# Moving the square and the upper-half copy of a weight conversion from ScalarE to GpSimd in a one-core attention and gated-MLP kernel

## The chip, the cores and the metric

The kernel runs on one core of one Trainium2 chip. The metric is the device time of one execution in microseconds (us), taken on the chip: the median of several runs. One further execution is recorded by the hardware profiler, and the profile and the trace come from that one. Engines are named as in the profile: PE (TensorE, the matrix engine, with PEld for its weight loads), DVE (VectorE), ACT (ScalarE), POOL (GpSimd) and SP (SyncE, which here only issues DMAs).

## The reference

Block-causal attention (8 batches, 8 heads, 576 positions, head size 64, blocks of 64) followed by a gated layer with 512 inputs and 1536 hidden columns:

```python
scores = scale * np.matmul(q, k.transpose(0, 1, 3, 2))
scores = np.where(mask, scores, -1000000000.0)      # mask: block_i >= block_j
scores = scores - np.max(scores, axis=-1, keepdims=True)
attn = np.exp(scores)
attn = attn / (np.sum(attn, axis=-1, keepdims=True) + 1e-09)
out = np.matmul(attn, v)
# x: out with heads joined, 4608 tokens x 512
gate = 1.0 / (1.0 + np.exp(-(x @ w_gate)))
val = x @ w_val
return (gate * val @ w_out).astype(np.float32)
```

The inputs of this case reach the core as 64-bit floating-point numbers for the three weight matrices, so the kernel reads each weight as two 32-bit words and makes 32-bit numbers of them itself.

## The kernel before, in words

**Two phases.** The first runs attention over 32 pairs of heads (`attend`, `prep`) and, interleaved on TensorE, the first 512 hidden columns of the gated layer (`mlp1`, four tiles of 128 columns, F1 = 4). The second does the other 1024 hidden columns. The change is in the first.

**One attention pair.** A pair is a list of steps (the tuples FIRST, ALONE, REST and TURN): scores of row block 3 and 2, the tail and the low blocks; for each a maximum on VectorE (line 385, or 425 for the tail) and exponentials on ScalarE (line 388, 427); transposes on TensorE (line 262) and their evictions from PSUM on ScalarE (line 363) or VectorE (line 489); the product with V on TensorE (line 258). The product, the division (line 507) and the split of the result into an upper and a lower part (line 514 on ScalarE, line 519 on GpSimd) of a pair are emitted within the next pair. `prep` makes the queries and keys of the next pair: for the first pairs with transposes on TensorE and evictions on ScalarE (lines 300 and 304), small copies on GpSimd (line 318); for the following ones with transposes on VectorE (line 290), scalings and copies on GpSimd (lines 343, 345, 329, 336).

**The conversion.** The operands of the large products are kept as an upper part of type float32r (`dH`) and the difference to it (`dL`). `convert` makes both from the 64-bit weights, a piece of 128 x 512 numbers at a time: eight pieces for the gate and value weights of the four hidden tiles, four for the output weights. Per piece it issues: the fetch (line 87 or 89, on the DMA queue of SyncE); shift and mask of the high word (line 111, VectorE); the square of the high word read as a float (line 113, ScalarE), which serves as a guard that sets tiny numbers to zero; the sign bits (line 114), the guard itself (line 116), the exponent (line 119) and the weight of the low word (line 120), all on VectorE; their sum (line 121, GpSimd); the rounded copy to the upper part (line 122, ScalarE); the difference as the lower part (line 123, GpSimd).

Buffers: for gate and value pieces the raw words and the intermediate `T_` have two buffers, the square (`cgv[:, 7]`) and the exponent (`cgv[:, 6]`) one each. For output pieces the raw words and the square (`csq`, which shares its two buffers with the tile `ost` of `mlp1`) have two, `T_` one.

**What sets the order.** CONV_PLAN says how many pieces are emitted in which pair: for gate and value two in pair 0 and one in each of pairs 1 to 6, for the output weights one in pairs 5 and 6 and two in pair 7. `mlp1` needs the two pieces of hidden tile f before its matmuls of that tile (line 131), and the four output pieces before those of line 138. The program's scheduler then orders each engine's instructions in its own model of time: of those that are ready it takes the one emitted first. `after` in `convert` ties an instruction behind the last attention instruction of its engine at the time of emission (`behind`, an order without a semaphore): the fetch on SyncE, line 111 on VectorE and line 113 on ScalarE are tied so. Lines 121 to 123 are not. The instructions of each engine stand in its queue in the order that results.

Of the kernel before, what the change touches and what calls it, by code (L numbers as in the profile page):

```python
# [9 lines left out]
F32 = mybir.dt.float32  # L10
F32R = mybir.dt.float32r
U32 = mybir.dt.uint32
AF = mybir.ActivationFunctionType
ALU = mybir.AluOpType
# [28 lines left out]
def attn_glu_kernel(ctx: ExitStack, tc: tile.TileContext, q, k, v, w_gate, w_val, w_out, out):  # L43
    nc = tc.nc
# [25 lines left out]
    def behind(ins, other):  # L70

        tc.add_manual_dep(ins, other.name, mybir.DependencyInfo(mybir.DependencyClass.NoSync,
                                                                mybir.DependencyReason.DATA), reason="order")

    def convert(pieces, tiles, last=None, ahead=False):

        def after(engine, ins):
            if last and engine in last:  # L80
                behind(ins.ins, last[engine])

        def fetch(i):
            src, (raw, *rest) = pieces[i][2], tiles(i)
            chunks = len(src.shape) == 3
            if chunks:
                dma = nc.sync.dma_start(out=raw.rearrange("p (c n) w -> p c (n w)", n=P), in_=src.bitcast(U32))
            else:
                dma = nc.sync.dma_start(out=raw, in_=src.bitcast(U32).rearrange("p (n w) -> p n w", w=2))
            after("SP", dma)  # L90
            return chunks, raw, *rest

        ready = [fetch(0)]
        yield
        if ahead:
            ready.append(fetch(1))
            yield
        for i, (dH, dL, src) in enumerate(pieces):
            chunks, raw, T_, E_, sq = ready.pop(0)
            if not ready and i + 1 < len(pieces):  # L100
                ready.append(fetch(i + 1))

            def like(t):
                return t.rearrange("p (c n) -> p c n", n=P) if chunks else t

            lo, hi = raw[:, :, 0], raw[:, :, 1]
            if E_ is None:
                E_ = hi
            Tf, Ef = T_.bitcast(F32), E_.bitcast(F32)

            after("DVE", nc.vector.tensor_scalar(out=T_, in0=hi, scalar1=3, scalar2=0x3FFFFFF8,
                                                 op0=ALU.logical_shift_left, op1=ALU.bitwise_and))
            after("ACT", nc.scalar.activation(out=sq, in_=hi.bitcast(F32), func=AF.Square))
            nc.vector.scalar_tensor_tensor(out=T_, in0=hi, scalar=0xC0000000, in1=T_,
                                           op0=ALU.bitwise_and, op1=ALU.bitwise_or)
            nc.vector.scalar_tensor_tensor(out=Tf, in0=sq, scalar=TINY_HI * TINY_HI, in1=Tf,
                                           op0=ALU.is_ge, op1=ALU.mult)

            nc.vector.tensor_scalar(out=E_, in0=T_, scalar1=0xFF800000, scalar2=None, op0=ALU.bitwise_and)
            nc.vector.scalar_tensor_tensor(out=Ef, in0=lo, scalar=2.0 ** -52, in1=Ef, op0=ALU.mult, op1=ALU.mult)  # L120
            nc.gpsimd.tensor_add(out=Tf, in0=Tf, in1=Ef)
            nc.scalar.copy(out=dH, in_=like(Tf))
            nc.gpsimd.tensor_sub(out=dL, in0=like(Tf), in1=dH.bitcast(F32))
            yield

# [38 lines left out]
    with ExitStack() as s2:  # L164
# [406 lines left out]
        def conv_out():  # L571
            W_out.append(mp.tile([P, F1, 2, DM], F32R, name="wo"))
            yield from convert([x for f in range(F1) for x in out_w(W_out[0], 0, f, DM)], tiles_o, last)

        conv_gv = convert([x for f in range(F1) for x in gate_val_chunks(wg, wv, f)], tiles_gv, last, ahead=True)
        conv_o = conv_out()
        n_conv = [-1, -1]
# [517 lines left out]
```

## Time and profile before

| | |
|---|---|
| median of 3 runs | 1180.55 us (1180.47 to 1180.87) |
| span of the profiled execution, first to last instruction | 1177.6 us |
| around that span, against the median | 2.95 us |
| DVE, ACT, POOL busy | 776.6, 617.4, 349.6 us |
| squares and copies of `convert` on ACT | 24, from 13.1 to 146.3 us |

Times in the trace count from the span's start. A row of the timeline reads: start, duration, engine, line, operation, output<-input, shape, count, and in brackets the idle time of the engine before it with what ended it. Durations of one engine may overlap a little, since the next instruction starts while the last one drains. A row of stages reads: the stretch, then the busy time of PE, PEld, DVE, ACT and POOL, the granted clock of TensorE (1.00 is full), the share of the DMA engines and GB/s. A row of one line reads: count, shortest/median/longest in ns, first and last start in us, and the shapes.

### The profile page before, as it was taken

Reading aid. Unit: us, or ns where it says so; the run is one execution under the profiler, and the core shown is the slowest. Engines: PE = TensorE matmul, PEld = TensorE weight load, DVE = VectorE, ACT = ScalarE, POOL = GpSimd, SP = SyncE. Lnnn points to the kernel's source line nnn. Section 1 sums busy time; section 2 is a strip of 40 time slices with the busy share of each in tenths; the row PEclk is TensorE's granted clock in tenths of the full one; section 3 lists DMA queues with packets and bytes.
Section 4 is the critical chain, followed back from the end, with each engine's and each line's share of the span. In section 5 each row is a group of like instructions: output and inputs, shape, how many; then the busy total and the mean of one; then the engine's idle time right before and its main releaser. Section 6 shows DMA issues by size and latency. Waiting matters only on the chain.

```text
span 1177.6 us, 19283 instructions
## 1 busy us (share of the span) xinstructions
PE 1153.6 (98%) x6749; PEld 976.3 (83%) x6749; DVE 776.6 (66%) x1405; ACT 617.4 (52%) x1364; POOL 349.6 (30%) x390
## 2 busy tenths in 40 slices
PE   6999999999999999999999999999999999999998
PEld 4555778778777877787889899999999998998997
DVE  5778845454564555457959977867877746746754
ACT  5867766766676676666334443553453422423421
POOL 2345523222331322234002133032033263262330
PEclk8999999999999999999999999999999999999999
DMA  8765434435434443534323236235197455164241
GB/s 198 180 144 115 104 89 100 117 74 127 99 89 112 102 122 71 125 105 134 111 95 126 91 120 223 71 136 202 39 339 276 158 172 179 39 212 132 83 143 54
DMA packets 253361, 153.34 MB, mean 130 GB/s; under 512 B 193232, under 2 KB 215248, under 8 KB 252624
## 3 DMA queue, kind: packets, MB, share of 16 engines
q1 hardware_dynamic: 241600, 132.15, 40.1%
q10 hardware_dynamic: 11280, 18.91, 4.4%
q8 instruction: 53, 0.87, 0.3%
q0 software_dynamic: 384, 1.05, 0.3%
q14 instruction: 44, 0.36, 0.1%
HBM read 104.73 MB, written 47.33 MB: 129 GB/s over the span
## 4 chain that ended last, share of the span: by engine, by line
PE 90%; DVE 5%; ACT 2%; issue 1%; DMA 1%; POOL 0%; SPq 0%; DVEq 0%; ACTq 0%
PE b L875 27%; PE bank L258 14%; PE m L131 14%; PE m L953 11%; PE m L138 7%; PE bank L262 6%; PE b L953 5%; PE bank L131 3%; ACT P L388 1%; PE m L262 1%; PE bank L138 1%; DVE nm L385 1%; DVE XL L765 0%; DMA raw<-in_moe_w_out_dram 0%; DMA rqk<-in_k_dram 0%
## 5 line engine op out<-in xcount | busy, mean ns | idle before, releaser
L875 PE MATMUL b<-XH,w 128*128 128x384 f32 x1344 | 349.2, 335 | 1.2 <-DVE g L921 1.2
L875 PEld LDWEIGHTS b<-XH,w 128*128 128x128 f32 x1344 | 243.9, 188 | 5.2 <-DVE g L921 1.6
L875 PE MATMUL b<-XL,w 128*128 128x384 f32 x672 | 223.5, 335 | 0.0
L388 ACT ACTIVATE P<-bank,nm 128x512 f32<-128x512 f32 (+3 forms) x256 | 132.1, 530 | 68.3 <-DVE nm L385 68.2
L385 DVE TENSOR_REDUCE nm<-bank 128x2 f32<-128x1024 f32 (+3 forms) x128 | 105.4, 823 | 40.7 <-ACT P L388 37.6
L875 PEld LDWEIGHTS b<-XL,w 128*128 128x128 f32 x672 | 126.1, 188 | 1.6
L953 PE MATMUL m<-wo,hH 128*128 128x512 f32 x384 | 125.0, 391 | 0.0
L363 ACT COPY G<-bank 128x768 f32<-128x768 f32 (+3 forms) x140 | 93.2, 694 | 26.2 <-PE bank L262 25.3
L258 PE MATMUL bank<-G,VS 128*64 128x320 f32 (+4 forms) x896 | 93.9, 360 | 0.1
L751 POOL TENSOR_TENSOR XB<-XB 128x384 f32<-128x384 f32 x20 | 20.7, 1037 | 237.9 <-DMA XB<-xT_d 191.6
L138 PE MATMUL m<-wo,hH 128*128 128x512 f32 x256 | 85.4, 398 | 1.4 <-ACT ost L632 1.0
L258 PEld LDWEIGHTS bank<-G,VS 128*64 128x64 f32 x896 | 55.9, 137 | 36.7 <-issue 4.3
L900 ACT ACTIVATE g<-g 128x384 f32<-128x384 f32 x72 | 37.8, 526 | 88.5 <-DVE g L913 48.6
L953 PEld LDWEIGHTS m<-wo,hH 128*128 128x128 f32 x384 | 72.0, 188 | 13.5
L131 PE MATMUL m<-XH,wv 128*128 128x512 f32 x240 | 82.3, 400 | 0.0
L131 PE MATMUL m<-XH,wg 128*128 128x512 f32 x240 | 82.1, 399 | 0.0
L764 ACT CAST XH<-XB 128x1536 fp32r<-128x1536 f32 (+2 forms) x72 | 65.2, 941 | 29.4 <-DVE XB L762 24.1
L765 DVE TENSOR_TENSOR XL<-XB,XH 128x1536 fp32r<-128x1536 f32 (+2 forms) x72 | 75.8, 1084 | 0.0
L262 PEld LDWEIGHTS bank<-ident,P 128*128 128x128 f32 x560 | 65.8, 141 | 11.5 <-ACT P L388 0.8
L953 PE MATMUL m<-wo,hL 128*128 128x512 f32 x192 | 75.2, 392 | 0.0
L262 PE MATMUL bank<-ident,P 128*128 128x128 f32 x560 | 74.8, 273 | 0.1
L409 DVE MEMSET bank<- 64x128 f32 x64 | 10.6, 165 | 88.0 <-PE bank L258 87.3
(183 smaller groups left out, 2339.5 us busy)
## 6 DMA issues: line engine op xcount, KB each, us to landing
xT_d<-xT ACTq DMA_DIRECT2D x32, 288.0 KB
XB<-xT_d SPq DMA_DIRECT2D x16, 576.0 KB
part_d<-ost SPq DMA_DIRECT2D x36, 256.0 KB
VS<-in_v_dram SPq DMA_DIRECT2D x64, 128.0 KB
part_d<-ost ACTq DMA_DIRECT2D x32, 256.0 KB
rqk<-in_k_dram SPq DMA_DIRECT2D x108, 72.0 KB
rqk<-in_q_dram SPq DMA_DIRECT2D x108, 72.0 KB
wgv_d<-st SPq DMA_DIRECT2D x8, 896.0 KB
```

What stands on the lines that cost most here:

```text
L131: mm = nc.tensor.matmul(ps, lhsT=lh, rhs=rh, start=(i == 0), stop=(i == n - 1))
L138: mm = nc.tensor.matmul(ps, lhsT=lh[:, f, t * P:(t + 1) * P], rhs=rh, start=(f == i == 0), stop=(f == F1 - 1 and i == 2))
L258: pe_last[:] = [nc.tensor.matmul(*args, **kw).ins]
L262: pe_last[:] = [nc.tensor.transpose(*args).ins]
L363: mark("ACT", nc.scalar.copy(out=dst, in_=src))
L385: mark("DVE", nc.vector.tensor_reduce(out=nm[:, c0:c0 + 2], in_=ps[:, :, c:c + n], axis=AX.X, op=ALU.max, negate=True))
L388: mark("ACT", nc.scalar.activation(out=Pi[:, h], in_=ps[:, h, c:c + n], func=AF.Exp, bias=nm[:, c0 + h:c0 + h + 1], accum_out=sm[:, 5 * h ...
L764: nc.scalar.copy(out=XO[j][0][:, a:b], in_=x)
L765: sub = nc.vector.tensor_sub(out=XO[j][1][:, a:b], in0=x, in1=XO[j][0][:, a:b].bitcast(F32))
L875: mm = nc.tensor.matmul(ps, lhsT=lh, rhs=rh, start=(first and k == 0), stop=(k == n - 1), skip_group_check=not first)
L900: mark2("ACT", nc.scalar.activation(out=t, in_=c, func=AF.Tanh, scale=0.5))
L953: mm = nc.tensor.matmul(po[t], lhsT=lh[:, f, t * P:(t + 1) * P], rhs=rh, start=(half == 0 and i == 0), stop=(half == 1 and i == 5))
```

## The change

The square of the guard and the copy to the upper part, in all twelve pieces, are issued on GpSimd. The square becomes a product of the high word with itself, and the tie behind the last attention instruction of ScalarE, which the square had, is dropped with nothing in its place. Nothing else is edited; the scheduler orders the program anew.

```diff
             after("DVE", nc.vector.tensor_scalar(out=T_, in0=hi, scalar1=3, scalar2=0x3FFFFFF8,
                                                  op0=ALU.logical_shift_left, op1=ALU.bitwise_and))
-            after("ACT", nc.scalar.activation(out=sq, in_=hi.bitcast(F32), func=AF.Square))
+            nc.gpsimd.tensor_tensor(out=sq, in0=hi.bitcast(F32), in1=hi.bitcast(F32), op=ALU.mult)
             nc.vector.scalar_tensor_tensor(out=T_, in0=hi, scalar=0xC0000000, in1=T_,
                                            op0=ALU.bitwise_and, op1=ALU.bitwise_or)
...
             nc.gpsimd.tensor_add(out=Tf, in0=Tf, in1=Ef)
-            nc.scalar.copy(out=dH, in_=like(Tf))
+            nc.gpsimd.tensor_copy(out=dH, in_=like(Tf))
             nc.gpsimd.tensor_sub(out=dL, in0=like(Tf), in1=dH.bitcast(F32))
```

## The prediction

> **What bounds the kernel now.** I read the page first: the span, the busy shares and the shares of the chain that ended last.
>
> ```profile
> span 1177.6 us, 19283 instructions
> PE 1153.6 (98%) x6749; PEld 976.3 (83%) x6749; DVE 776.6 (66%) x1405; ACT 617.4 (52%) x1364; POOL 349.6 (30%) x390
> PE 90%; DVE 5%; ACT 2%; issue 1%; DMA 1%; POOL 0%; SPq 0%; DVEq 0%; ACTq 0%
> ```
>
> TensorE is busy for 98% of the span and carries 90% of the chain. The three runs have a median of 1180.55 us, so 2.95 us lie around the profiled span of 1177.6; I hold these fixed and sum against the median. What happens beside a busy TensorE costs nothing unless TensorE then waits. The edit touches twelve pieces (eight of the gate and value weights, four of the first output weights), so next I read the stages that hold them.
>
> ```profile
> 40.00:60.00 20.00, 18.23 (x138) 12.12 (x137) 14.37 (x30) 16.70 (x54) 6.77 (x9) 1.00 0.73 170
> 150.00:600.00 450.00, 449.12 (x2936) 356.75 (x2937) 260.40 (x501) 286.47 (x689) 119.44 (x161) 1.00 0.44 109
> ```
>
> After 150 us TensorE is idle for under 1 us in 450. Before it, in attention pairs such as those of 40 to 60 us, TensorE waits 1.8 us in 20, ScalarE is busy for 16.7 and VectorE for 14.4: the pair is a ring of short waits, and a delay of any engine in the ring is a delay of everything behind it. So the edit can act only ahead of 150 us, and what it gains or loses there shifts the rest unchanged.
>
> **The change, part by part. What moves.** The costs, as count: shortest/median/longest ns, from the views of single lines.
>
> ```profile
> L113 ACT ACTIVATE cgv<-cgv x8: 658/672/702, 13.1 to 105.8; 128x512 f32<-128x512 f32 x8
> L122 ACT CAST wg<-cgv x4: 612/618/642, 18.3 to 98.3; 128x512 fp32r<-128x512 f32 x4
> L121 POOL TENSOR_TENSOR cgv<-cgv x8: 1263/1270/1287, 16.4 to 111.2; 128x512 f32<-128x512 f32 x8
> L601 POOL CAST XH<-XH x1: 734/734/734, 553.3 to 553.3; 128x256 fp32r<-128x256 f32 x1
> L336 POOL CAST QBL<-QL x48: 227/234/245, 117.2 to 524.5; 64x64 fp32r<-64x64 f32 x48
> ```
>
> ScalarE loses a square of 0.67 and a copy of 0.62 us per piece: 12 x 1.29 = 15.5 us. GpSimd gains a product of two 128x512 operands, which I price as its sum of that shape, 1.27 us. The copy of 512 elements to fp32r has no row; the nearest casts take 0.234 us for 64 elements and 0.734 for 256, which is 2.6 ns an element, so 0.734 + 256 x 2.6 = 1.40 us. It cannot be below 0.734 and should not pass twice that, 1.47. GpSimd gains 12 x 2.67 = 32 us. The Trainium skill, GPSIMD Engine Reference, section Engine selection, puts one-input operations there at roughly line rate (its section on elementwise cost measures a loop of 512 elements at 0.769 us): by it the copy would be 0.77 us and the last term below +0.1 instead of +0.7 at its worst; the two cast rows speak against it, and the 1.40 stands.
>
> **The queues.** On GpSimd the sum, the copy and the difference of a piece now follow each other with no wait for another engine, 1.27 + 1.40 + 1.28 us in one block. Behind the block stand copies and scalings for the next attention pair, which are wanted some 10 us later. The square had an order constraint on ScalarE; on GpSimd it has none, so it goes as early as its data and its one buffer allow. The data are early, as fetches already are: the two first pieces of the output weights are fetched at 31.48, in the third of 32 pairs.
>
> ```profile
> 31.48 1.07 SPq L89 DMA_DIRECT2D XB<-in_moe_w_out_dram  x2
> ```
>
> The buffer of the squares of gate and value pieces is single, and free when line 116 of the piece before has read it. So I expect the square of piece i+1 on GpSimd right after line 116 of piece i, while VectorE has lines 119 and 120 of piece i still to do. Line 116 itself will not wait: its square is a pair old. No DMA is issued by the moved steps.
>
> **One pair in detail (47 us).** ScalarE, VectorE and GpSimd:
>
> ```profile
> 47.09 0.67 ACT L113 ACTIVATE cgv<-cgv 128x512 f32<-128x512 f32 x1
> 48.12 0.68 ACT L514 CAST XH<-xT 128x576 fp32r<-128x576 f32 x1
> 51.85 0.60 ACT L300 ACTIVATE KQ<-m 128x512 f32<-128x512 f32 x1 [0.85 <-PE m L262]
> 52.34 0.68 ACT L388 ACTIVATE P<-bank,nm 128x512 f32<-128x512 f32 x1
> 48.24 0.69 DVE L116 SCALAR_TENSOR_TENSOR cgv<-cgv 128x512 f32<-128x512 f32 x1
> 49.16 1.41 DVE L119 TENSOR_SCALAR cgv<-cgv 128x512 uint32<-128x512 uint32 x1
> 50.49 1.21 DVE L385 TENSOR_REDUCE nm<-bank 128x2 f32<-128x1024 f32 x1
> 48.88 1.41 POOL L519 TENSOR_TENSOR XL<-xT,XH 128x576 fp32r<-128x576 f32 x1 [6.02 <-ACT XH L514]
> ```
>
> The maximum (line 385) is ready at 51.70, the exponential that needs it starts at 52.34, because line 300 stands before it. ScalarE is late by 0.64 us, and the square's slot (47.09 to 47.66) is 0.57 of that. Taken out, the exponential starts at 51.77: -0.57 us. The other side is line 119: it takes 0.42 us undisturbed and 1.41 here, because the GpSimd subtraction of line 519 runs from 48.88. VectorE and GpSimd do not overlap in these instructions; about 1 us is the price of one GpSimd instruction meeting one of VectorE's. The Trainium skill, SBUF — State Buffer, section Who interferes with whom, says why: a VectorE instruction with two SBUF inputs, or in a two-port mode, and a GpSimd instruction lock each other out for the whole instruction. The trace agrees (+0.99 us), and this is the rule that speaks against the change.
>
> Now line 519 waits only for line 514, which comes 0.57 earlier, so it starts at 48.3, level with line 116 at 48.24. If line 116 is first, the square falls mainly under the maximum, which reads PSUM and was not stretched (1.21): the pair gains 0.57. If line 519 is first, line 116 waits until some 49.6 and ends at 50.3; then the square starts at once, line 119 follows 0.23 us later (49.16 less the end of line 116, 48.93) and waits about 1 us; the maximum ends near 52.9 and the exponential is 0.6 later than now. This pair: -0.57 or +0.6, taken as 0.
>
> The pairs before and after it:
>
> ```profile
> 35.42 0.69 DVE L116 SCALAR_TENSOR_TENSOR cgv<-cgv 128x512 f32<-128x512 f32 x1
> 37.59 1.21 DVE L385 TENSOR_REDUCE nm<-bank 128x2 f32<-128x1024 f32 x1
> 39.28 0.68 ACT L388 ACTIVATE P<-bank,nm 128x512 f32<-128x512 f32 x1
> 35.82 1.56 POOL L519 TENSOR_TENSOR XL<-xT,XH 128x576 fp32r<-128x576 f32 x1 [6.20 <-ACT XH L514]
> 61.13 0.69 DVE L116 SCALAR_TENSOR_TENSOR cgv<-cgv 128x512 f32<-128x512 f32 x1
> 64.60 0.69 ACT L388 ACTIVATE P<-bank,nm 128x512 f32<-128x512 f32 x1 [1.54 <-DVE nm L385]
> 61.53 1.55 POOL L519 TENSOR_TENSOR XL<-xT,XH 128x576 fp32r<-128x576 f32 x1 [5.60 <-ACT XH L514]
> ```
>
> At 35 us line 519 moves from 35.82 to 35.25, ahead of line 116 at 35.42: the second order. ScalarE's slack was 39.28 - 38.80 = 0.48, so the net is between -0.2 (no square behind) and +0.65; taken +0.6. At 61 us line 519 moves to 60.96, again ahead of 61.13. ScalarE waits 1.54 us for VectorE there, so nothing is gained: +0.2 to +1.0, taken +0.9. The three pairs together: +1.5.
>
> **The start.** The square of the first piece and the one at 19.57:
>
> ```profile
> 13.12 0.70 ACT L113 ACTIVATE cgv<-cgv 128x512 f32<-128x512 f32 x1
> 13.86 0.69 DVE L116 SCALAR_TENSOR_TENSOR cgv<-cgv 128x512 f32<-128x512 f32 x1 [1.68 <-ACT cgv L113]
> 19.57 0.66 ACT L113 ACTIVATE cgv<-cgv 128x512 f32<-128x512 f32 x1
> 20.65 1.11 PE L262 MATMUL m<-ident,rqk 128*128 128x128 f32 x4 [3.00 <-ACT G L363]
> 19.50:20.00 0.50, 0.00 (x0) 0.00 (x0) 0.50 (x1) 0.50 (x3) 0.50 (x1) 0.50 0.83 185
> 29.50:30.00 0.50, 0.50 (x5) 0.40 (x6) 0.00 (x0) 0.34 (x2) 0.13 (x1) 0.96 0.61 171
> ```
>
> VectorE waits 1.68 us for the first square; without that, lines 116, 425, 119 and 120 come earlier and the second softmax block with them: 0.57 us for the slot of the square, some 0.6 for VectorE's wait. The second square's slot, up to 0.55, lies right ahead of the eviction for which TensorE waits 3.00 us. TensorE would resume some 1.7 us earlier, near 18.9. But the granted clock fell to half near 19.3 and came back near 29.5; if it comes back when it did, 1.7 us of work that ran at full clock now runs at half, which gives back a third to a half. Bounds -1.8 and -0.6; taken -1.2.
>
> **Later pairs.**
>
> ```profile
> 78.27 1.23 DVE L385 TENSOR_REDUCE nm<-bank 128x2 f32<-128x1024 f32 x1
> 79.43 0.62 ACT L122 CAST wv<-cgv 128x512 fp32r<-128x512 f32 x1 [1.73 <-POOL cgv L121]
> 79.97 0.68 ACT L388 ACTIVATE P<-bank,nm 128x512 f32<-128x512 f32 x1
> 96.99 0.69 ACT L388 ACTIVATE P<-bank,nm 128x512 f32<-128x512 f32 x1 [2.60 <-DVE nm L385]
> 112.52 0.62 ACT L122 CAST wv<-cgv 128x512 fp32r<-128x512 f32 x1 [0.94 <-POOL cgv L121]
> 114.58 1.21 PE L258 MATMUL bank<-KQ,QB 128*128 128x288 f32 x4 [1.36 <-issue]
> ```
>
> At 79.43 the copy, late for want of GpSimd's sum, holds the exponential until 79.97, though the maximum was ready at 79.50: -0.45 without it, +0.75 for the square meeting line 119: +0.3. At 112.52 the same (-0.45), and there is no next square; TensorE's 1.36 us wait at 114.58 follows from that exponential. At 96.99 ScalarE waits 2.60 us for VectorE, so only the collision counts, 0 to +0.9, taken +0.5. Together +0.35.
>
> **The last output piece.**
>
> ```profile
> 145.00 1.30 POOL L121 TENSOR_TENSOR XB<-XB 128x512 f32<-128x512 f32 x1 [0.63 <-DVE XB L120]
> 147.01 0.50 PE L138 MATMUL m<-wo,hH 128*128 128x512 f32 x1 [0.25 <-ACT wo L122]
> ```
>
> TensorE waits 0.25 us at 147.01 for ScalarE's copy of the last piece, right behind the sum of 145.00 to 146.31. On GpSimd the copy ends at 147.7 instead of 146.96: +0.7, or 0 where the pieces ahead finish earlier because their copies no longer wait in ScalarE's queue; taken +0.4.
>
> **Sum:** -1.2 + 1.5 + 0.35 + 0.4 = +1.05, that is 1180.55 + 1.05 = 1181.6 us. The bounds of the terms (start -1.8 to -0.6, the three pairs -0.57 to +2.25, later -0.9 to +0.75, last 0 to +0.7) rarely meet at one end. What a measurement of this kernel can tell from no change is 0.2%, 2.4 us. So the forecast is: no change that can be told, 1179.5 to 1183.5.
>
> **Rivals.** *The squares miss VectorE (faster).* If they are queued where VectorE reads PSUM (before the pair's line 111, or under the maximum), the pairs give -0.2, -0.57 and +0.2, the later ones -0.9, and with the start and the last piece the sum is -2.3: 1178.3. For it: GpSimd is idle in most of a pair. Against it: the buffer comes free just at line 116. Chance 0.22.
>
> *The clock holds (faster).* The half clock covered 19.3 to 29.5, behind a wait of 3.00 us. With that wait nearer 2.2 us, or with the recovery one step earlier, TensorE does some 5 of those 10 us of work in half the time: another -2.5, so 1179.1. Against it: TensorE is then still idle for over 2 us at that place. Chance 0.13.
>
> *GpSimd is backed up when VectorE converts (slower).* The place is lines 114 to 120 in the five pairs from 34 to 97 us: with a second GpSimd instruction waiting behind line 519 each time, be it a square of this kind of weights or one of the output weights, VectorE is locked out twice per piece. The price, on top of the forecast: the pairs at 47 and 90 us at their worse ends (+0.6 and +0.4), and one more meeting in each of the five, 0.9 less the 0.23 of other work between two such lines, 5 x 0.67 = 3.35; in all +4.35, 1185.9. It decides as soon as GpSimd's queue holds two ready instructions when line 114 begins. Chance 0.15.
>
> *The relief never reaches the path.* ScalarE's freed 15.5 us all fall where it waits for maxima anyway, and the collisions fall beside TensorE's work: 1180.5. Chance 0.05.
>
> **How the numbers follow.** The forecast keeps 0.45. Faster by over 2.4 us takes half of the first rival (0.11), somewhat under half of the second (0.06) and 0.05 of the forecast: 0.22. Slower takes most of the third (0.13) and three tenths of the forecast (0.14): 0.27. The rest, 0.51, is no change. Range: 1177.6, where both faster rivals partly hold, to 1186.0, which is the slower one.
>
> **What would show it.** Right: on GpSimd a product of 1.27 us directly after line 116 of the piece before, a copy near 1.4; more of lines 116, 119 and 120 stretched past 1.3 us than now; the exponentials of the pairs at 47 and 79 us no longer behind lines 300 and 122; TensorE back before 19.5 us. Wrong: the products far from line 116, a copy near 0.8, no new stretched lines, a half clock that is gone or short, or a changed order of the attention work, which the program's scheduler makes anew and which I cannot see from here.

## The result and the profile after

| kernel | median of its runs | runs |
|---|---|---|
| before | 1180.51 us (1177.65 to 1180.87) | 4 |
| after | 1186.76 us (1185.66 to 1187.78) | 4 |

The changed kernel takes 1.006 of the time of the one before (95% interval 1.0045 to 1.0074): it is slower by 0.6%, 6.25 us, and lies 0.8 us above the predicted range. The profiled execution took 1185.66 us, 1.76 us of it outside the span. Other executions on record have about as much outside theirs, so of the 2.95 us that were set beside the span before, some 1.2 us is an estimate of how far that profiled execution lay below its median. The two profiles differ by 6.3 us, as the medians do.

First the page of the changed kernel (span and busy shares).

```profile
span 1183.9 us, 19282 instructions
PE 1155.7 (98%) x6749; PEld 977.8 (83%) x6749; DVE 778.3 (66%) x1405; ACT 605.1 (51%) x1340; POOL 369.8 (31%) x414
```

Then its views of line 113 and line 122 (count, shortest/median/longest ns, first and last start).

```profile
L113 POOL TENSOR_TENSOR cgv<-cgv x8: 1041/1068/1433, 7.8 to 93.6; 128x512 f32<-128x512 f32 x8
...
L122 POOL CAST wg<-cgv x4: 610/611/611, 13.1 to 97.8; 128x512 fp32r<-128x512 f32 x4
```

The moved work is cheaper on GpSimd than I had priced it: 0.61 us a copy and 1.04 to 1.07 us a square. GpSimd is busy for 20.2 us more (369.8 less 349.6), not for 32. The kernel is slower all the same, so the price of the work is not what decides.

Where the time went is seen in the table of stages, which gives per stretch the busy time of PE, PEld, DVE, ACT and POOL and then the granted clock. Before:

```profile
0.00:40.00 40.00, 29.19 (x155) 17.95 (x155) 23.56 (x48) 25.19 (x70) 10.49 (x24) 0.87 0.83 198
40.00:100.00 60.00, 54.99 (x356) 35.58 (x356) 47.31 (x91) 43.93 (x123) 25.15 (x26) 1.00 0.63 143
100.00:135.00 35.00, 33.20 (x224) 23.00 (x224) 26.86 (x52) 28.14 (x75) 18.19 (x19) 1.00 0.48 111
135.00:160.00 25.00, 23.60 (x162) 17.84 (x159) 17.86 (x32) 16.73 (x39) 12.70 (x16) 1.00 0.46 110
```

The same stretches after:

```profile
0.00:40.00 40.00, 29.52 (x165) 18.11 (x166) 24.26 (x51) 24.15 (x72) 17.04 (x31) 0.96 0.82 199
40.00:100.00 60.00, 52.22 (x344) 33.67 (x342) 47.69 (x87) 37.02 (x104) 34.19 (x35) 1.00 0.61 141
100.00:135.00 35.00, 34.26 (x222) 24.24 (x222) 24.78 (x47) 24.76 (x67) 20.75 (x24) 0.96 0.49 113
135.00:160.00 25.00, 20.90 (x127) 14.88 (x124) 19.97 (x36) 13.39 (x33) 14.24 (x18) 0.86 0.38 84
```

TensorE loses a stretch's length less its busy time (it idles), and its busy time times what the clock lacks of 1.00 (it works at half speed for part of it). From 0 to 40 us that is 10.81 + 29.19 x 0.13 = 14.6 us before and 11.7 after: a gain of 2.9, mainly in the clock. From 40 to 100 us it is 5.0 and 7.8, a loss of 2.8; from 100 to 135, 1.8 and 2.1; from 135 to 160, 1.4 and 4.10 + 20.90 x 0.14 = 7.0, a loss of 5.6. The four make +5.8 of the 6.1 us by which all later pairs are shifted. So there are three things to explain: a gain at the start, a loss of some 3 us in the pairs with gate and value pieces, and a loss of over 5 us in one place around 145 us.

For all kernels I use one ruler: the start of the product with V (line 258, `bank<-G,VS`) in each pair, less its start in the kernel before. In the pairs that stand at 133.7 and 152.2 us in the kernel before, the rows of the changed kernel are these.

```profile
134.59 2.93 PE L258 MATMUL bank<-G,VS 128*64 128x320 f32 x28
158.33 1.03 PE L258 MATMUL bank<-G,VS 128*64 128x320 f32 x6
```

That is +0.9 at the first and +6.1 at the second, and from there on the shift hardly changes in any kernel (by 0.3 us at most up to the end, in e11 by 0.9). Each row of the table is one execution, the profiled one, and the level at the start is not the edit's alone: e12 has the order of the kernel before on TensorE, VectorE, ScalarE and GpSimd up to 107 us and stands at +1.2 there all the same, and e2 and e10, with the same order up to 112 us, stand at +1.2 and -1.6 at 30 us. So it is the steps along a row that are read, more than its levels. In e11 the product at 134 us runs in two parts, at 130.43 and 135.74; the table has the first.

| us later than before, in the pair at | 30 | 43 | 56 | 70 | 86 | 103 | 119 | 134 | 152 | end |
|---|---|---|---|---|---|---|---|---|---|---|
| after | -1.8 | -2.0 | -0.7 | +0.1 | -0.3 | +2.2 | +1.5 | +0.9 | +6.1 | +6.3 |
| e1, squares alone | -0.3 | +0.8 | +1.2 | +3.6 | +4.3 | +5.2 | +6.0 | +6.0 | +6.8 | +7.0 |
| e2, copies alone | +1.2 | +1.2 | +1.2 | +1.0 | +0.7 | +0.7 | +0.3 | +0.8 | +5.9 | +6.0 |
| e3, after + tied squares | -1.7 | -1.5 | -1.1 | -1.1 | -1.5 | -1.5 | -2.4 | -2.4 | +1.7 | +1.8 |
| e4, tie in output pieces only | -0.3 | +0.2 | +0.6 | +2.7 | +3.1 | +5.6 | +4.8 | +4.7 | +8.8 | +9.1 |
| e5, e3 with output copies on ScalarE | -2.6 | -2.8 | -2.1 | -2.2 | -2.6 | -2.6 | -3.5 | -2.3 | -0.7 | -0.6 |
| e6, e3 with two T_ | -2.2 | -2.2 | -1.1 | -1.1 | -1.5 | -1.5 | -1.7 | -2.2 | +0.5 | +0.7 |
| e7, gate and value pieces only | -2.6 | -1.5 | -1.1 | +1.2 | +1.5 | +3.9 | +3.2 | +3.5 | +3.4 | +3.4 |
| e8, output pieces only | +0.3 | +1.0 | +0.5 | +0.5 | +0.5 | +0.5 | +1.0 | +0.6 | +4.6 | +4.7 |
| e9, e3 in gate and value pieces only | -0.3 | -0.3 | +0.1 | +0.1 | -0.3 | -0.3 | -1.2 | -0.9 | -0.9 | -0.8 |
| e10, e2 with an added order | -1.6 | -0.5 | -0.5 | -0.7 | -1.0 | -1.0 | -1.5 | +1.3 | +0.7 | +0.9 |
| e11, e3 with an added order | -2.6 | -2.3 | +1.0 | +1.0 | +0.6 | +0.6 | -0.3 | -3.2 | +1.8 | +2.7 |
| e12, before with two T_ | +1.2 | +1.2 | +1.2 | +1.2 | +1.2 | +1.2 | +2.6 | +6.5 | +5.1 | +5.4 |

The step from 134 to 152 us is the clearest in it: every kernel with the output pieces' copies on GpSimd and no order added loses 2.7 to 5.2 us there (after, e2, e3, e4, e6, e8); those with only their squares on GpSimd lose 0.8 and 1.6 (e1, e5); those that leave the output pieces as they were lose nothing (e7, e9).

### The profile page after: what moved, and what is told of

Read it like the earlier page. It is cut to its first block, busy times and chain, and to the rows that moved or that the text cites. A ratio compares the mean times of both kernels' runs of the same rounds, so it can differ in the third digit from the quotient of the medians.

```text
span 1183.9 us, 19282 instructions
## 1 busy us (share of the span) xinstructions
PE 1155.7 (98%) x6749; PEld 977.8 (83%) x6749; DVE 778.3 (66%) x1405; ACT 605.1 (51%) x1340; POOL 369.8 (31%) x414
## 3 DMA queue, kind: packets, MB, share of 16 engines
q0 software_dynamic: 384, 1.05, 0.3%
## 4 chain that ended last, share of the span: by engine, by line
PE 91%; DVE 3%; DMA 2%; issue 1%; ACT 1%; SPq 1%; POOL 0%; DVEq 0%; ACTq 0%; POOLq 0%
PE b L875 29%; PE m L131 14%; PE bank L258 14%; PE m L953 11%; PE m L138 7%; PE bank L262 6%; PE b L953 5%; PE bank L131 3%; PE bank L138 1%; ACT P L388 1%; DVE nm L385 1%; SPq L228 0%; PE m L262 0%; DMA XB<-in_moe_w_out_dram 0%; DMA r_d<-rT 0%
## 5 line engine op out<-in xcount | busy, mean ns | idle before, releaser
L329 POOL TENSOR_SCALAR KQ<-KQ 128x128 f32<-128x128 f32 x24 | 13.3, 556 | 177.6 <-DVE KQ L290 177.6
```

## The experiments

Medians are compared with runs of the kernel before on the same chip. The theories at first: by the *queue theory* (from e5 on, the *order theory*) the loss comes from where the moved instructions stand in GpSimd's queue: squares right behind line 116, and the difference of an output piece too far back. By the *load theory* it comes from the time that they take on GpSimd, wherever they stand. By the *ScalarE theory* it is ScalarE's new order.

| | median us | before us | ratio (95%) |
|---|---|---|---|
| e1 | 1185.01 | 1179.55 | 1.0049 (1.0037 to 1.0062) |
| e2 | 1183.45 | 1179.55 | 1.0033 (1.0021 to 1.0046) |
| e3 | 1182.25 | 1179.55 | 1.0021 (1.0013 to 1.003) |
| e4 | 1186.71 | 1179.55 | 1.006 (1.0046 to 1.0074) |
| e5 | 1180.17 | 1179.17 | 1.001 (1.0001 to 1.0018) |
| e6 | 1180.41 | 1179.17 | 1.0013 (1.0004 to 1.0021) |
| e7 | 1181.98 | 1179.17 | 1.0026 (1.0015 to 1.0038) |
| e8 | 1183.56 | 1179.17 | 1.0034 (1.0022 to 1.0046) |
| e9 | 1178.19 | 1179.68 | 0.9986 (0.9978 to 0.9995) |
| e10 | 1180.88 | 1179.68 | 1.0011 (1.0002 to 1.0019) |
| e11 | 1181.34 | 1179.68 | 1.0012 (1.0003 to 1.0021) |
| e12 | 1184.74 | 1179.68 | 1.0037 (1.0024 to 1.0051) |

**e1 and e2: each half alone.** e1 keeps the copy on ScalarE, e2 the square (with its tie):

```diff
e1:
-            nc.gpsimd.tensor_copy(out=dH, in_=like(Tf))
+            nc.scalar.copy(out=dH, in_=like(Tf))
e2:
-            nc.gpsimd.tensor_tensor(out=sq, in0=hi.bitcast(F32), in1=hi.bitcast(F32), op=ALU.mult)
+            after("ACT", nc.scalar.activation(out=sq, in_=hi.bitcast(F32), func=AF.Square))
```

> Only the square on GpSimd, the copy on ScalarE. Queue theory (the loss comes from the place of the square in GpSimd's queue: ahead of line 123 while its own words are still on the way, and beside line 119): nearly the whole loss, 1184.5 to 1187. Load theory (the loss grows with GpSimd's added busy time, 12.5 us from squares and 7.3 us from copies): about two thirds, 1183.5 to 1185. ScalarE theory (the relief was worth something and the copy lost it): under 1182.

> Only the copy on GpSimd, the square on ScalarE with its tie. Queue theory: no loss, 1179.5 to 1181.5, since the copy stands between the sum and the difference and holds nobody up. Load theory: a third of the loss, 1182 to 1183.

Measured: 5.5 and 3.9 us more than before. Both halves cost by themselves, and at different places: e1 loses its 6 us step by step up to 134 us, e2 its 5 us in the one step after it. The queue theory, which had put all of the loss on the squares, missed e2: there is a second cause. The load theory, with 1185 and 1183 as its upper ends, was nearer to both. The ScalarE theory falls with e1.

**e3 and e4: the square's place.** The square is ordered behind the difference (line 123) of the piece before, in all pieces or in the output pieces alone. Nothing is taken off GpSimd.

```diff
-            nc.gpsimd.tensor_tensor(out=sq, in0=hi.bitcast(F32), in1=hi.bitcast(F32), op=ALU.mult)
+            square = nc.gpsimd.tensor_tensor(out=sq, in0=hi.bitcast(F32), in1=hi.bitcast(F32), op=ALU.mult)
...
+            if i: behind(square.ins, lower.ins)
...
-            nc.gpsimd.tensor_sub(out=dL, in0=like(Tf), in1=dH.bitcast(F32))
+            lower = nc.gpsimd.tensor_sub(out=dL, in0=like(Tf), in1=dH.bitcast(F32))
e4:
+            if i and not chunks: behind(square.ins, lower.ins)
```

> The changed kernel with each square tied on GpSimd's queue behind line 123 of the piece before. Queue theory: the squares meet neither line 119 nor a difference that waits, so the loss goes: 1179.5 to 1181.5. Load theory: same GpSimd work, 1185.5 to 1187.5.

> The same tie for the four pieces of the output weights alone. Queue theory: the lag that arises behind 124 us (from +1.7 to +6.1) goes, the one before it stays: 1181.5 to 1183.5. Load theory: 1185.5 to 1187.5.

e3 is 2.7 us above the kernel before and not 6.25; at 134 us it is even 2.4 us ahead. e4 is as slow as the changed kernel, where the load theory had it and the queue theory had not; the place of the output pieces' squares is not what their loss comes from. What e3 saves and e4 does not belongs to the place of the gate and value squares. How, is seen in the timeline of one pair. After, VectorE from line 111 to the maximum (line 385), with GpSimd:

```profile
45.88 0.42 DVE L111 TENSOR_SCALAR cgv<-cgv 128x512 uint32<-128x512 uint32 x1
...
47.12 1.72 DVE L116 SCALAR_TENSOR_TENSOR cgv<-cgv 128x512 f32<-128x512 f32 x1
49.07 1.18 DVE L119 TENSOR_SCALAR cgv<-cgv 128x512 uint32<-128x512 uint32 x1
50.16 1.21 DVE L385 TENSOR_REDUCE nm<-bank 128x2 f32<-128x1024 f32 x1
...
46.75 1.54 POOL L519 TENSOR_TENSOR XL<-xT,XH 128x576 fp32r<-128x576 f32 x1 [2.07 <-ACT XH L514]
48.92 1.04 POOL L113 TENSOR_TENSOR cgv<-cgv 128x512 f32<-128x512 f32 x1 [0.63 <-DVE cgv L116]
```

The same pair in e9 (below), where gate and value squares are tied as in e3:

```profile
46.89 0.42 DVE L111 TENSOR_SCALAR cgv<-cgv 128x512 uint32<-128x512 uint32 x1
...
48.14 1.70 DVE L116 SCALAR_TENSOR_TENSOR cgv<-cgv 128x512 f32<-128x512 f32 x1
50.07 0.40 DVE L119 TENSOR_SCALAR cgv<-cgv 128x512 uint32<-128x512 uint32 x1
50.40 1.19 DVE L385 TENSOR_REDUCE nm<-bank 128x2 f32<-128x1024 f32 x1
```

Line 116 is held up by line 519 in both. Line 119 is held up only where the square stands right behind line 116: 1.18 us against 0.40. From line 111 to the maximum it takes 4.28 us against 3.51, 0.77 more for this one meeting. In a later pair the meeting has a consequence of its own. After:

```profile
94.04 1.26 DVE L119 TENSOR_SCALAR cgv<-cgv 128x512 uint32<-128x512 uint32 x1
...
93.60 1.42 POOL L113 TENSOR_TENSOR cgv<-cgv 128x512 f32<-128x512 f32 x1 [1.32 <-DVE cgv L116]
...
99.12 1.90 PE L258 MATMUL bank<-KQ,QB 128*128 128x288 f32 x4 [1.94 <-ACT P L388]
```

TensorE in e9, and then the stage from 100 to 105 us after the change:

```profile
98.21 1.21 PE L258 MATMUL bank<-KQ,QB 128*128 128x288 f32 x4 [1.10 <-POOL wg L122]
```

```profile
100.00:105.00 5.00, 5.00 (x24) 3.56 (x24) 2.88 (x6) 3.49 (x8) 3.58 (x4) 0.71 0.80 136
```

TensorE waits 1.94 us where it waits 1.10 in e9, and then has a mean clock of 0.71 from 100 to 105 us: that is 5.00 x 0.29 = 1.45 us more, an estimate from this row. The 0.84 of the wait and the 1.45 are nearly all of the ruler's step of +2.5 from 86 to 103 us; e9 has no step there.

**e7 and e8: the two kinds of pieces.** The whole change, untied, in the gate and value pieces alone (e7) or in the output pieces alone (e8); the other kind has lines 113 and 122 as before.

```diff
e7 (e8 with "not chunks"):
+            nc.gpsimd.tensor_tensor(out=sq, in0=hi.bitcast(F32), in1=hi.bitcast(F32), op=ALU.mult) if chunks else after("ACT", nc.scalar.activation(out=sq, in_=hi.bitcast(F32), func=AF.Square))
...
+            (nc.gpsimd.tensor_copy if chunks else nc.scalar.copy)(out=dH, in_=like(Tf))
```

> The change in the eight gate and value pieces alone (untied squares, copies on GpSimd); the four output pieces as before. Order theory: the two losses are apart. What the gate and value pieces cost is there by 134 us (the changed kernel was +0.9 us at that point), and no jump follows: 0 to 2 us more than the kernel before. Load theory: eight of twelve pieces bring two thirds of the loss of 6.3 us: 4.2 us more.

> The change in the four output pieces alone; the gate and value pieces as before. Order theory: the jump between 134 and 152 us is whole: 4 to 6 us more than the kernel before (nothing gained at the start either). Load theory: four of twelve pieces bring one third of the loss of 6.3 us: 2.1 us more.

Measured: 2.8 and 4.4 us more. The four output pieces cost more than the eight others, against the load theory, and they do so in the one step after 134 us. e7 came out 0.8 us above what the order theory allowed; its eight executions lie between 1179.75 us, at a mean granted clock of 1.000, and 1184.98, at 0.994, so that whether a half-clock stretch follows differs here from one execution to the next.

**What happens at 145 us.** After the change, GpSimd, VectorE, ScalarE and TensorE around the third and fourth output pieces:

```profile
140.78 0.61 POOL L122 CAST wo<-XB 128x512 fp32r<-128x512 f32 x1
142.26 0.53 POOL L336 CAST QBH<-QH 64x64 fp32r<-64x64 f32 x2 [0.36 <-ACT QH L328]
142.88 1.68 POOL L123 TENSOR_TENSOR wo<-XB,wo 128x512 fp32r<-128x512 f32 x1
...
144.59 0.43 DVE L111 TENSOR_SCALAR XB<-XB 128x512 uint32<-128x512 uint32 x1 [1.18 <-POOL wo L123]
145.78 1.79 DVE L116 SCALAR_TENSOR_TENSOR XB<-csq,XB 128x512 f32<-128x512 f32 x1
147.67 1.32 DVE L119 TENSOR_SCALAR XB<-XB 128x512 uint32<-128x512 uint32 x1
148.91 1.21 DVE L385 TENSOR_REDUCE nm<-bank 128x2 f32<-128x1024 f32 x1
...
151.74 0.61 PE L258 MATMUL bank<-KH,QBH 128*128 128x288 f32 x1 [3.38 <-ACT P L388]
```

And before:

```profile
135.98 1.28 POOL L123 TENSOR_TENSOR wo<-XB,wo 128x512 fp32r<-128x512 f32 x1 [1.28 <-ACT wo L122]
137.58 0.54 POOL L329 TENSOR_SCALAR KQ<-KQ 128x128 f32<-128x128 f32 x1 [0.32 <-DVE KQ L290]
...
137.34 0.38 DVE L111 TENSOR_SCALAR XB<-XB 128x512 uint32<-128x512 uint32 x1
145.14 1.22 DVE L385 TENSOR_REDUCE nm<-bank 128x2 f32<-128x1024 f32 x1
```

Before, the difference of the third piece stood ahead of lines 329 and 336 of the next pair; after, it stands among them, between the two copies of line 336. It frees the only `T_` of the output pieces.

That is not the whole delay. The sum of the third piece starts at 139.40 us after and at 133.41 before, so most of the delay is there already, and part of it comes from the second piece's difference. After:

```profile
133.40 1.04 POOL L113 TENSOR_TENSOR csq<-XB 128x512 f32<-128x512 f32 x1 [2.98 <-DMA XB<-in_moe_w_out_dram]
134.40 1.27 POOL L123 TENSOR_TENSOR wo<-XB,wo 128x512 fp32r<-128x512 f32 x1
...
135.71 0.43 DVE L111 TENSOR_SCALAR XB<-XB 128x512 uint32<-128x512 uint32 x1 [1.98 <-POOL wo L123]
```

Before:

```profile
127.54 1.30 POOL L123 TENSOR_TENSOR wo<-XB,wo 128x512 fp32r<-128x512 f32 x1
...
128.88 0.43 DVE L111 TENSOR_SCALAR XB<-XB 128x512 uint32<-128x512 uint32 x1 [0.47 <-POOL wo L123]
```

The fourth piece's untied square stands ahead of the second piece's difference and waits 2.98 us for its fetch; the difference waits behind it, and line 111 of the third piece waits for the difference. That square alone does not decide either. In e3 the tie puts each square behind a difference; by the ruler e3 is 2.4 us ahead at 134 us, but its third sum starts at 133.42 us, no earlier than before the change, and its third difference, among the same lines, at 137.37 instead of 135.98. In e2, with its squares on ScalarE, lines 116 to 120 of the third piece stand behind a maximum for which VectorE waits 3.61 us, and follow from 135.70 us on. What these kernels share is that the differences of the output pieces come later, and with them the piece behind; the place among lines 329 and 336 is the last part of it.

So, after the change, line 111 of the fourth piece starts at 144.59 and not at 137.34, four of that piece's five VectorE lines stand in one block right ahead of the next maximum, two of them stretched by GpSimd, and the maximum is at 148.91 instead of 145.14. TensorE waits 3.38 us for the exponential behind it, and is then at a clock of 0.86 on the mean of 135 to 160 us.

**e5, e6 and e10: three ways to mend it.** e5 is e3 with the output pieces' copies on ScalarE; e6 is e3 with two buffers for their `T_`; e10 is e2 with nothing but an order: line 329 behind the last difference, up to that of the third output piece (`lowers` lists the differences as they are emitted).

```diff
e5:
+            (nc.gpsimd.tensor_copy if chunks else nc.scalar.copy)(out=dH, in_=like(Tf))
e6:
-            return (co[0][:, j:j + 1024].rearrange("p (n w) -> p n w", w=2), co[1][:, :512], None,
+            return (co[0][:, j:j + 1024].rearrange("p (n w) -> p n w", w=2), co[1][:, 512 * (i % 2):512 * (i % 2) + 512], None,
e10:
-                nc.gpsimd.tensor_scalar_mul(KQ[:, 1, :P], KQ[:, 1, :P], scale)
+                behind(nc.gpsimd.tensor_scalar_mul(KQ[:, 1, :P], KQ[:, 1, :P], scale).ins, lowers[min(len(lowers), 11) - 1])
```

> e3 with one edit: the copies of the four output pieces are back on ScalarE; the copies of gate and value and all squares stay on GpSimd, the squares tied as in e3. Order theory: the loss between 134 and 152 us comes from the place of the third output piece's difference (line 123), which with the copy on GpSimd stands behind the next pair's lines 329 and 336; with the copy on ScalarE it stands ahead of them again, so the jump of +4 us goes and the lead of 2.4 us that e3 has at 134 us lasts to the end: 2.4 us less than the kernel before (1.0 to 3.0 less), a ratio of 0.998. Load theory: the loss is the time that the copies and products take on GpSimd and in which VectorE is locked out; of that 0.61 x 4 us goes back to ScalarE, so the time stays within 1 us of e3: 1.5 to 2.7 us more than before.

> e3 with one edit: the output pieces get two buffers for the intermediate T_, so line 111 of the fourth piece does not wait for the difference of the third. The orders on TensorE and SyncE are those of e3, on GpSimd nearly (line 123 of the third piece still behind lines 329 and 336); only VectorE's changes. Order theory by way of the buffer: lines 111 and 114 of the fourth piece run early, the maximum ahead of which they stood starts 1.5 to 3.5 us earlier, and the time is 1 to 2.5 us less than before. If the rest of the block (lines 116, 119, 120 and the two lockouts) is enough to delay the maximum, half of it stays: about the kernel before. TensorE theory: the loss is in the new order of lines 138 and 262 on TensorE, which stays: e3's time, 2.7 us more than before. Load theory: the same as e3.

> e2 (copies alone on GpSimd) with one added order: line 329 of a pair stands on GpSimd behind the last difference (line 123) emitted, up to that of the third output piece. Nothing is taken off GpSimd. The scheduler then puts line 111 of the third output piece under the maxima again, as before the change. Order theory: the jump of 5 us between 134 and 152 us goes: 0 to 1.5 us more than the kernel before. Load theory: the copies take as long as in e2, so e2's 3.9 us more stay.

Measured: +1.0, +1.2 and +1.2 us. e10 speaks most plainly against the load theory: the copies take as long on GpSimd as in e2, and 2.7 of e2's 3.9 us are gone by an order alone (which makes the scheduler change the order on the other engines too). In e2:

```profile
140.17 0.53 POOL L329 TENSOR_SCALAR KQ<-KQ 128x128 f32<-128x128 f32 x1
142.14 1.29 POOL L123 TENSOR_TENSOR wo<-XB,wo 128x512 fp32r<-128x512 f32 x1
```

In e10:

```profile
135.28 1.29 POOL L123 TENSOR_TENSOR wo<-XB,wo 128x512 fp32r<-128x512 f32 x1
136.70 1.06 POOL L329 TENSOR_SCALAR KQ<-KQ 128x128 f32<-128x128 f32 x1
```

The step from 134 to 152 us, +5.0 in e2, is -0.6 in e10. But e10 has a new loss one pair earlier, +2.8 from 119 to 134 us, where the added order brings TensorE to a wait that e2 hasn't:

```profile
128.17 0.37 PE L258 MATMUL bank<-KH,QBH 128*128 128x288 f32 x1 [1.95 <-ACT P L388]
```

The granted clock is 0.66 from 130 to 135 us behind it. From 119 to 152 us e10 so loses 2.2 us and e2 5.6; the rest of their distance in the table was there at 30 us, while their orders were still the same.

The order theory's sizes were too good, though. It had expected e5 at 2.4 us less than before. In e5 the difference is back ahead of line 329, but a square still stands between the two, and line 111 of the fourth piece meets it:

```profile
135.73 1.05 POOL L113 TENSOR_TENSOR csq<-XB 128x512 f32<-128x512 f32 x1
...
135.85 1.21 DVE L111 TENSOR_SCALAR XB<-XB 128x512 uint32<-128x512 uint32 x1
```

1.21 us instead of 0.38. And the profiled execution of e5, 0.6 us ahead of the kernel before, was the fastest of its eleven. In e6, 2.7 of e3's 4.0 us between 134 and 152 us remain. The second buffer lets line 111 of the fourth piece run at 131.71, but e6 also keeps the tie, so the fourth piece's square stands behind the third piece's difference, and line 116 waits for the square:

```profile
141.66 0.69 DVE L116 SCALAR_TENSOR_TENSOR XB<-csq,XB 128x512 f32<-128x512 f32 x1 [1.90 <-POOL csq L113]
```

So e6 takes one of two ways away by which the difference holds up the fourth piece, and does not tell what the wait for `T_` is worth alone. TensorE's order in e6 is that of e3 throughout, so the 1.3 us less between 134 and 152 us are not a matter of that.

**e9, e11 and e12: the change without its losses, and a control.** e9 has the change with tied squares in the gate and value pieces, and the output pieces as before. e11 is e3 with the order of e10: all 24 instructions on GpSimd, and both losses meant to go. e12 is the kernel before with the two buffers of e6.

> The change with tied squares in the eight gate and value pieces alone; the four output pieces as in the kernel before. In e5 the fourth output piece's square still stood on GpSimd at 135.73 us and line 111 met it (1.21 us instead of 0.38), which is 0.8 of the 1.5 us that ScalarE was ahead there. Order theory: with that square on ScalarE nothing is lost between 134 and 152 us, and the lead of 1.5 to 2.4 us stays: 1.5 us less than the kernel before (0.7 to 2.4 less). Load theory: 16 of the 24 moved instructions still load GpSimd; not below the kernel before, 0.5 to 2 us more.

> e3 (the whole change, squares tied behind the difference of the piece before) with the added order of e10: all 24 instructions stay on GpSimd. Order theory: both losses go and the gain of the start stays: 0 to 2.4 us less than the kernel before. Load theory: e3's 2.7 us more stay.

> A control for e6: the kernel before with two buffers for T_ of the output pieces. In its trace line 111 of the fourth piece waits for nothing (137.34 us), so by the order theory the second buffer brings nothing here: within 1 us of the kernel before. If it is 1.5 us less, the gain of e6 over e3 is the buffer's own and says nothing of the change.

e9 gave what was expected: 1.5 us less than the kernel before (interval 0.6 to 2.6 us), so it beats both kernels; at 134 us it is 0.9 ahead in its profile and stays so. It also makes the cleanest pair of all: e7 and e9 have the same order on TensorE, VectorE and ScalarE from the first instruction to the last, and differ on GpSimd alone, in where the gate and value squares stand. That place is worth 2.8 + 1.5 = 4.3 us. e11 is 1.7 us slower than before, not faster. In its profiled execution it is 2.3 us ahead at 43 us and 1.0 behind at 56, with a mean clock of 0.94 between 40 and 100 us; why that stretch of half clock comes is open. It meets the wait that e10 has, too:

```profile
129.35 0.37 PE L258 MATMUL bank<-KH,QBH 128*128 128x288 f32 x1 [1.95 <-ACT P L388]
```

From 145 to 160 us TensorE idles 1.5 us in e11 and 1.4 before, both at full clock, so the loss at 145 us is gone there; the added order has put another in its place.

e12 missed most, and says most. It adds no work anywhere and takes a possible wait away, and is 5.1 us slower. With a second `T_` the fourth piece's lines run at once behind the third's:

```profile
129.21 1.27 DVE L111 TENSOR_SCALAR XB<-XB 128x512 uint32<-128x512 uint32 x1
...
132.29 1.59 DVE L116 SCALAR_TENSOR_TENSOR XB<-csq,XB 128x512 f32<-128x512 f32 x1
...
135.23 1.21 DVE L385 TENSOR_REDUCE nm<-bank 128x2 f32<-128x1024 f32 x1
```

Four of the piece's lines (111, 114, 116 and 119, with 1.27, 1.67, 1.59 and 1.33 us) are stretched by GpSimd's work and stand ahead of a maximum, which in the kernel before starts at 127.00 us. It is the loss of 145 us again, one pair earlier and with nothing moved to GpSimd; another 1.4 us of step comes from 103 to 119 us. By these timelines, what costs is a piece's block of VectorE lines between GpSimd's instructions and ahead of a maximum, whichever edit brings it there; no run moves that block alone. It also follows that e6 can't be read as "the buffer alone" for a second reason: the buffer changes the order by itself.

## Why the prediction was wrong

The sum was +1.05 us, the result +6.25. Step by step:

- *What bounds the kernel, and where the edit can act*: right. From 160 to 1170 us TensorE is busy for 1008.67 us after and 1008.77 before, and the shift no longer changes.
- *What moves*: the copy was mis-sized, 0.61 us where I took 1.40 and called 0.734 the lowest possible. The casts that I scaled have 64 and 256 elements, and the one of 512 is shorter than that of 256. The one row of 256 (0.734, at 553.29 us) ran beside VectorE's line 754, which ended at 553.78, so it may hold a meeting like those priced in the same prediction; no run shows that cast undisturbed. The rule of the Trainium skill (GPSIMD Engine Reference, section Engine selection: one-input operations at roughly line rate), which I had turned down for those rows, was on the right side. (With the 0.77 us that the prediction set beside it, its last term would have been +0.12, not "below +0.1".) The square was 1.04 and not 1.27. Both errors made the change look dearer than it was, and it was slower nevertheless.
- *The queues*: the squares' place was right in three of the eight gate and value pieces, directly behind line 116, 0.08 us after its end in the pair at 47 us. "As early as its data allow" had a price that was not foreseen: six of the twelve squares stand at the head of GpSimd's queue before their words are there, with waits of up to 7.84 us (at 36.29 us). e4, which ties the output squares, is no faster, so this does not decide. **The step that failed** is the other sentence, that the sum, the copy and the difference follow each other in one block with no wait, and that behind it stand copies "which are wanted some 10 us later". I had asked who waits behind the block, and not what comes in between. With the copy on GpSimd the scheduler puts lines 329 and 336 between the third output piece's copy and its difference, and a square that waits for its fetch between the second's; and the difference is what line 111 of the next output piece waits for. In place of a block with no wait, the runs show +4.0 to +5.2 us between 134 and 152 us where the copies of the output pieces are on GpSimd (e8, e3, e4, e2 and after). Before the change that wait did not show: the difference ended at 137.26 us and line 111 began at 137.34.
- *The last output piece*: taken +0.4 with bounds of 0 and +0.7, for TensorE's wait for the last copy at 147.01 us. Measured: +5.2 (after), +5.1 (e2), +4.0 (e8). The term had the right place and the wrong waiter: it was the maximum ahead of that copy that came late, by 3.8 us, and the half clock behind it cost about as much as TensorE's added waiting (2.9 and 2.7 us in the stage from 135 to 160).
- *The pairs at 35, 47 and 61 us*: taken +1.5 together. The ruler goes from -1.8 at 30 us to +0.1 at 70 us, +1.9. The mechanism, the double meeting that was described, is there at 47 and 61 us; that the sum is near is in part luck, since the pairs came out at -0.2, +1.3 and +0.8 where +0.6, 0 and +0.9 were taken. One more meeting was priced at 0.67 us in the third rival and is worth 0.77 in the pair at 47 us.
- *Later pairs*: taken +0.35, measured -0.4, +2.5 and -0.8 in the pairs at 79, 97 and 112 us (the ruler's steps from 70 to 119 us), +1.4 together. The meeting at 97 us was foreseen (0 to +0.9); the half clock behind it was not.
- *The start*: taken -1.2 within -1.8 and -0.6, measured -1.8 in the one profile. The eight profiles with the gate and value squares and copies on GpSimd lie between -2.6 and -0.3 at 30 us, the three with both on ScalarE (before, e8, e12) between 0 and +1.2, so the gain is shown, but its size only roughly. The assumption that the clock would come back when it did, near 29.5 us, was wrong, as the stage after the change shows:

```profile
25.00:30.00 5.00, 4.76 (x33) 3.34 (x35) 2.77 (x6) 4.16 (x14) 2.99 (x5) 1.00 0.55 169
```

  The rival in which the clock holds was half right, and its gain was lost again by 103 us.

Of the rivals, that GpSimd is backed up when VectorE converts (1185.9 us) came nearest in size. Its place, 34 to 97 us, bore +4.0 by 103 us in the ruler (from -1.8 to +2.2), near its 4.35, though a good part by the half clock; but the start's gain had paid for some of that, and the loss that decides, the step after 134 us, has another cause. Its number was near by chance.

The first theory of the runs fell too: it held the squares for the whole cause. What is shown now: the place of the untied gate and value squares (e7 against e9, whose orders differ in nothing else) and the late difference of the output pieces (e2, e3, e8, e10) are two separate causes, and the sixteen gate and value instructions save some 1.5 us net on GpSimd if both are avoided (e9). What stays open: what is left of e5, 1.0 us above the kernel before, of which the meeting at 135.85 us is a part; of e10 and e11, 1.2 and 1.7 us above, the wait of 1.95 us that the added order brings is a part. How the second cause divides between the wait for `T_`, the lockouts of VectorE and the half clock is not shown run by run.

## What to carry to other kernels

When work is moved to another engine, follow the last instruction of the moved chain in the new queue, see what can get in between it and its forerunner, and ask which buffer it frees and who waits for that buffer; what the instruction costs is the smaller question. In a kernel whose order a scheduler makes, an edit is a new order: here a second buffer alone cost 5 us. If a moved instruction is wanted in a certain place, tie it there: with the gate and value squares untied the edit cost some 3 us (e7), and with them behind the difference the same work saved 1.5 us (e9).

## What the runs showed of the hardware

A rounding copy of 128x512 to fp32r took 0.61 us on GpSimd, less than one of 128x256 in the kernel before (0.734, beside a VectorE instruction), and about as long as on ScalarE (0.618). The product of a tile with itself took 1.04 us, the sum of two tiles of that shape 1.27.

The length of TensorE's wait alone did not tell whether the clock falls. Behind 1.94 us (after, at 99.12) it fell to 0.71 on the mean of 100 to 105 us; behind 2.39 us in e6 (at 147.40) it stayed at 1.00 up to 155 us. The two rows of e10 and e11 above come closest to a pair: the same matmul, the same wait of 1.95 us, and then a clock of 0.66 from 130 to 135 us in e10 and of 1.00 in e11.

The Trainium skill, TensorE: Matmul & The Clock Gate, section on the HAM clock gate, says that activity is judged in windows of about 3.4 us that run freely; where a wait lies in them would then matter as well as its length. These waits agree with that, and no run here varies the place alone.
